# Two-layer mixer behind windowed attention: another order for the first tiles, the first weights and the next block's scores

## The chip, the cores and the metric

The kernel runs on one core of a Trainium2 chip. The metric is the time of one execution on the device in microseconds, the median of several runs. A profiled execution is taken apart, and its trace is what the views show: TensorE (PE, its weight loads PEld), VectorE (DVE), ScalarE (ACT), GpSimd (POOL) and SyncE (SP, which only issues transfers here).

## What is computed

Attention with a causal window of 64 over 4 batches, 8 heads, 576 positions and 64 channels; then two MLP blocks on rows of 512:

```
scores = where(0 <= i - j < 64, q @ k.T / 8, -1e9)
x  = softmax(scores) @ v                        # (4, 576, 512)
xn = (x - mean) / sqrt(var + 1e-6) * g_ln
x  = x + relu(xn @ w_ch1) @ w_ch2               # block "a": 512 -> 2048 -> 512
u  = x + (relu(x.T @ w_tok1) @ w_tok2).T        # over the 576 positions
out = u + relu(u @ w_ch1') @ w_ch2'             # block "b": 512 -> 1536 -> 512
```

All is float32 at the interface. In the MLPs a float32 product is made of three products in a faster format: each operand is split into a high part and a low rest, and high x high, high x low and low x high are summed.

## The kernel before, in words

The 2304 rows lie in 18 tiles of 128. Three tiles make a block of 384 rows, six blocks in all. A tile's attention is done in two units (half of the heads each); unit u belongs to tile u // 2.

The stages of a tile's attention have letters in the string FIRST, which gives the order in which the first three tiles' instructions are issued. S is a tile's scores (L179, 32 small TensorE matmuls into two PSUM tiles, then on VectorE for each unit four masked copies with their maxima, L190), and in the kernel before it ends with the exponentials of both units on ScalarE (`att_E`, L198, four with their sums). T transposes a unit's probabilities on TensorE (L211) and ScalarE copies them out of PSUM (L215) while GpSimd makes the reciprocals of the sums (L217, L218); U does the same with VectorE for the copy (L213) and for the reciprocals (L220, L221). V multiplies with the values (L263) and scales (L265, VectorE). L makes a tile's mean and variance (L271, L272 on VectorE, L273, L274 on GpSimd), N subtracts the mean (L290, VectorE), X transposes the tile's first three column chunks on TensorE (L300) and Y the fourth of all three tiles. E moves a chunk out of PSUM as high part (ScalarE, L317) and low part (VectorE, L318).

Weights come as pieces of 512 KB, in an integer view of 64 bit per value. Sixteen hidden chunks f have two pieces each: (f, 0) for the first product (mm1) and (f, 1) for the second (mm2). A piece goes through four steps: a transfer into one of six raw buffers (L426; the first six on SyncE's queue, the others on ScalarE's), `shrink` on ScalarE (L100; k in FIRST), `narrow` on VectorE (L110, then L113; n), and `split`, with the high part on ScalarE (L92) and the low part on GpSimd (L93; s). Each split issues the transfer of a later piece.

Block 0 of "a" runs over f: mm1 of f (12 matmuls, L351), the narrowing of two pieces, the relu and split of the result (L340 on ScalarE, L341 on VectorE), a list of hooks, then mm2 of f - 2 (nine matmuls, L364). The hooks hold the splits of the two pieces just narrowed, the shrinking of the next two, and the attention of tiles 3 to 5, which are the next block's. Every engine works off its own instructions in the order in which they are issued; the order is written out by hand, and what waits blocks what is behind it on its engine. From block 1 on no weights are prepared until the last block of "a".

Ten products of zeros keep TensorE at work at the very start (`WARM`).

Of the kernel before, what the change touches and what calls it, by code (L numbers as in the profile page):

```python
# [17 lines left out]
P = 128  # L18
# [17 lines left out]

FIRST = ("S0 T0 U1 S1 V0 V1 L0 T2 U3 S2 N0 X0 V2 V3 L1 T4 U5 N1 X1 n1 V4 V5 L2 n1 N2 X2 Y0 s0 E0 E1 E2 E3 k2")


WARM = 10
# [17 lines left out]
def mixer_kernel(ctx, tc, qT, kT, v, g, wa1, wa2, tok1, tok2, wb1, wb2, out):  # L60
# [100 lines left out]
    def att_S(t, lean, first=False):  # L161


        (ba, ia), (bb, _) = tile_blocks(t)
        m_ = masks[:, 1 if ia == 0 else 0]
        wide = [P, NH, 2 * BLK]
        s_ = [ps_a.tile(wide, F32, tag="a", name=f"s{2 * t + hh}") for hh in range(2)]
        for h in range(NH):
            c = slice(h * BLK, (h + 1) * BLK)
            for hh in range(2):  # L170
                r = slice(64 * hh, 64 * hh + 64)
                for s in range(2):
                    if s == 0 and ia == 0:

                        k_ = K[t][r, 1:2, c].to_broadcast([64, 2, BLK])
                    else:
                        j = s if ba == bb else 2 * s
                        k_ = K[t][r, j:j + 2, c]
                    nc.tensor.matmul(s_[hh][64 * s:64 * s + 64, h], lhsT=Q[t][r, s, c], rhs=k_, start=True, stop=True)  # L179
        for hh in range(2):  # L180
            u = 2 * t + hh
            if first:
                f_ = scratch[:, u % KD]
            else:
                f_ = sp.tile(wide, F32, tag="s", name=f"f{u}") if lean else whole[t][:, hh]
            probs[u] = f_
            mx = peak[u] = stp.tile([P, NH, 1], F32, tag="mx", name=f"mx{u}")
            norm[u] = stp.tile([P, NH, 1], F32, tag="sm", bufs=4, name=f"sm{u}") if lean else sums[t][:, hh]
            for h in range(NH):
                nc.vector.tensor_tensor_reduce(out=f_[:, h], in0=s_[hh][:, h], in1=m_, scale=-(D ** -0.5),  # L190
                                               scalar=-2.0 * MASK, op0=ALU.add, op1=ALU.min, accum_out=mx[:, h])
            if lean:
                att_E(u)

    def att_E(u):
# [187 lines left out]
    with tc.manual_schedule():  # L383
# [31 lines left out]
        nc.scalar.activation(out=warm, in_=mhalf, func=AF.Exp)  # L415


        tmps = wslot(FA - 1, [P, 4, DM], "tmps", U32)
        todo = [(0, 0)] + [x for f in range(FA - 1) for x in ((f + 1, 0), (f, 1))] + [(FA - 1, 1)]
        place_of = {x: k for k, x in enumerate(todo)}  # L420
        ready, raws = [], {}

# [14 lines left out]

        def wpairs(n):
            wshrink(n)
            pairs = []  # L440
            for x in ready[:n]:
                k = place_of[x]
                if k < 2 * FA - 3:
                    tmp = tmps[:, k % 4]
                else:
                    tmp = sp.tile([P, DM], U32, tag="s", name=f"tmp{k}")
                pairs.append((tmp, raws.pop(x)))
            return pairs

        def wnarrow(n=1):  # L450
            narrowed.extend((f, i, w) for (f, i), w in zip(ready[:n], narrow(wpairs(n))))
# [12 lines left out]
        for op in LOADS.split():  # L464
            {"q": load_qk, "v": load_v, "g": lambda _: nc.sync.dma_start(out=gsb, in_=g), "w": lambda n: wload(n, nc.sync)}[op[0]](int(op[1:]))

        def first_X(j, c):
            trans_tiles("a", xh, 0, c, (j,), ps_h if c == KD - 1 else ps_acc)

        fns = {"S": lambda t: att_S(t, True, True), "T": lambda u: att_T(u, True),  # L470
               "U": lambda u: att_T(u, True, nc.vector.tensor_copy), "V": att_PV,
               "L": ln_stats, "N": ln_center, "k": wshrink, "n": wnarrow, "s": lambda _: wsplit(False),
               "X": lambda j: [first_X(j, c) for c in range(KD - 1)],
               "Y": lambda _: [first_X(j, KD - 1) for j in range(TPB)], "E": lambda c: evac(c)}
        scratch = xnp.tile([P, KD, NH, P], F32, tag="xn", name="scratch")
        for op in FIRST.split():
            if op == "s0":
                xnt = xnp.tile([P, KD, 2, N], F32R, tag="xn", name="xnt")
            fns[op[0]](int(op[1:]))
        xn = [xnt[:, c] for c in range(KD)]  # L480
# [116 lines left out]
        for i in range(NBLOCKS):  # L597
            hooks = {f: [] for f in range(FA + 2)}
            if i < NBLOCKS - 1:
                u0 = 2 * TPB * (i + 1)  # L600
                lean = i == 0

                def next_qk(t):
                    if t + 1 < NT:
                        place_fixed(t + 1)
                        load_qk(t + 1)

                def next_v(t):
                    if t + 1 < NT:
                        load_v(t + 1)  # L610

                for k in range(2 * TPB if lean else 0):
                    def s1(u=u0 + k):
                        if u % 2 == 0:
                            new_x(u // 2)
                            att_S(u // 2, True)
                            next_qk(u // 2)

                    def s3(u=u0 + k):
                        att_PV(u)  # L620
                        if u % 2 == 1:
                            next_v(u // 2)
                            ln_stats(u // 2)

                    u, t = u0 + k, (u0 + k) // 2
                    hooks[2 * k].append(s1)
                    hooks[2 * k + 2].insert(0, lambda u=u: att_T(u))
                    hooks[2 * k + 3].append(s3)
                    if k % 2 == 1:
                        hooks[2 * k + 4].append(lambda t=t: ln_center(t))  # L630

                def step(op, t, n):
                    if op == "S":
                        new_x(t)
                        tile_S(t)
                        next_qk(t)
                    elif op == "V":
                        tile_PV(t)
                        next_v(t)
                        ln_scalar(t)  # L640
                    else:
                        (tile_T_part if op == "T" else xh_part)(t, n)

                done = collections.Counter()
                for f, ops in enumerate(() if lean else STEPS):
                    for op in ops.split():
                        what, _, n = op.partition("*")
                        for _ in range(int(n or 1)):
                            hooks[f].append(lambda a=(what[0], TPB * (i + 1) + int(what[1]), done[what]): step(*a))
                            done[what] += 1  # L650

                def tr3(i=i):
                    for c in range(3):
                        trans("a", xh, i + 1, c)
                if lean:
                    hooks[FA - 1].append(tr3)

                def after(i=i):
                    if i > 0:
                        for c in range(KD):  # L660
                            for j in range(TPB):
                                gained(c, slice(j * P, (j + 1) * P), uts[TPB * (i + 1) + j][:, c])
                    else:
                        for c in range(3):
                            evac(c)
                        trans("a", xh, i + 1, 3)
                        evac(3)
            else:
                def ysk(k):
                    new_ys(0, k)  # L670
                    for t in range(2 * k, min(2 * k + 2, 9)):
                        y_split(t, nc.vector)
                hooks[0].append(lambda: b_load(3))
                for k in range(5):
                    hooks[k + LAG + 1].append(lambda k=k: ysk(k))
                for f in range(6 + LAG, 13 + LAG):
                    hooks[f - 0.5] = [b_narrow]
                    hooks[f].append(b_split)
                    if f != 7 + LAG:
                        hooks[f] += [b_narrow, b_shrink]  # L680
                hooks[13 + LAG].append(b_split)

                def after():
                    pass
            if i == 0:
                for f in range(FA):
                    if f < FA - 2:
                        hooks[f - 0.5] = [lambda: wnarrow(2)]
                    hooks[f] = hooks[f][:1] + [wsplit] + hooks[f][1:] if f % 2 == 0 else [wsplit] + hooks[f]
                hooks[FA - 2].append(lambda: wnarrow(2))  # L690
            acc = mlp_block("a", i, W, FA, xn, hooks, after)
            for j in range(TPB):
                t = TPB * i + j
                nc.vector.scalar_tensor_tensor(out=xt[t], in0=acc[j], scalar=mv.pop(t)[:, 1:2], in1=xt[t],
                                               op0=ALU.mult, op1=ALU.add)
# [151 lines left out]
```

## Time and profile before

| | us |
|---|---|
| median of three runs | 851.88 |
| the runs | 851.76, 851.88, 854.1 |
| profiled execution | 854.01 |
| its span, first to last instruction | 851.9 |
| TensorE busy | 829.5 (97%) |
| VectorE busy | 525.6 (62%) |
| ScalarE busy | 282.2 (33%) |
| GpSimd busy | 122.5 (14%) |

The busy time of an engine is the time in which one of its instructions runs, waits inside the instruction included. The profiled execution's own time is the span and 2.1 us around it. Time in the trace starts with the span.

### The profile page before, as it was taken

How to read it: one execution, taken by the hardware profiler on the slowest of the kernel's cores; microseconds unless marked ns; L12 is line 12 of the kernel's file. 1: busy time of each engine (PE TensorE's matmuls, PEld its weight loads, DVE VectorE, ACT ScalarE, POOL GpSimd, SP SyncE). 2: the span in 40 equal slices, each digit the busy share in tenths (PEclk: the TensorE clock that was granted, in tenths of full speed). 3: DMA queues.
4: the chain of work that ended last, by engine and by line, in shares of the span. 5: the costliest groups of instructions: out<-in, count | busy, mean ns of one | idle time of the engine just before them, and what ended most of it. 6: DMA issues, size and time to landing. Idle time of an engine off the chain costs nothing.

```text
span 851.9 us, 12974 instructions
## 1 busy us (share of the span) xinstructions
PE 829.5 (97%) x4994; PEld 730.4 (86%) x4994; DVE 525.6 (62%) x1313; ACT 282.2 (33%) x759; POOL 122.5 (14%) x141
## 2 busy tenths in 40 slices
PE   7689999999999999999999999999999999999997
PEld 5578888888888888889999877798999999899996
DVE  4689957787777778777637737985443333344311
ACT  5567634323523432342235431433111111111110
POOL 3365520000000000000004441532000000000000
PEclk9789999999999999999999999999999999999999
DMA  9368512101110110203005400440101010010101
GB/s 328 126 221 266 204 39 79 51 26 63 57 50 26 56 57 25 68 27 99 1 1 155 161 0 25 173 124 0 38 1 38 1 38 0 1 38 1 38 1 37
DMA packets 23213, 58.37 MB, mean 69 GB/s; under 512 B 2800, under 2 KB 3568, under 8 KB 23152
## 3 DMA queue, kind: packets, MB, share of 16 engines
q1 hardware_dynamic: 19408, 43.92, 15.7%
q10 hardware_dynamic: 3744, 13.63, 4.6%
q8 instruction: 39, 0.64, 0.3%
q14 instruction: 22, 0.18, 0.1%
HBM read 52.82 MB, written 4.72 MB: 68 GB/s over the span
## 4 chain that ended last, share of the span: by engine, by line
PE 93%; DVE 3%; issue 1%; ACT 1%; POOL 1%; DVEq 0%; POOLq 0%; ACTq 0%
PE acca L364 24%; PE ha L351 23%; PE hb L351 17%; PE accb L364 17%; PE td L728 2%; PE s L179 2%; PE o L263 2%; PE th L712 1%; DVE ut L326 1%; ACT scratch L198 1%; PE idle L389 1%; PE pt L211 1%; PE king_offset=None)_1_4947 L712 0%; PE king_offset=None)_1_5092 L712 0%; PE king_offset=None)_1_4912 L712 0%
## 5 line engine op out<-in xcount | busy, mean ns | idle before, releaser
L351 PE MATMUL ha<-xnt,wa 128*128 128x384 f32 x1152 | 221.2, 341 | 4.3 <-ACT wa L92 2.4
L351 PEld LDWEIGHTS ha<-xnt,wa 128*128 128x128 f32 x1152 | 206.9, 190 | 13.1 <-ACT wa L92 2.7
L364 PE MATMUL acca<-wa,hTa 128*128 128x512 f32 x864 | 216.8, 397 | 0.0
L364 PEld LDWEIGHTS acca<-wa,hTa 128*128 128x128 f32 x864 | 159.4, 188 | 32.7 <-issue 1.7
L364 PE MATMUL accb<-wb,hTb 128*128 128x512 f32 x648 | 159.1, 392 | 0.0
L364 PEld LDWEIGHTS accb<-wb,hTb 128*128 128x128 f32 x648 | 120.7, 188 | 22.5
L341 DVE SCALAR_TENSOR_TENSOR hTb<-hb,hTb 128x384 fp32r<-128x384 f32 x72 | 40.1, 557 | 150.3 <-ACT hTb L340 150.2
L340 ACT ACTIVATE hTb<-hb 128x384 fp32r<-128x384 f32 x72 | 35.4, 492 | 238.6 <-PE hb L351 238.6
L340 ACT ACTIVATE hTa<-ha 128x384 fp32r<-128x384 f32 x96 | 46.8, 487 | 198.8 <-PE ha L351 198.6
L341 DVE SCALAR_TENSOR_TENSOR hTa<-ha,hTa 128x384 fp32r<-128x384 f32 x96 | 53.1, 554 | 87.6 <-ACT hTa L340 86.0
L239 DVE STREAM_TRANSPOSE pts<-f 32x256 f32<-32x256 f32 x192 | 83.6, 435 | 2.8
L351 PE MATMUL hb<-xnt,wb 128*128 128x384 f32 x432 | 80.9, 337 | 1.1 <-POOL wb L93 0.7
L351 PE MATMUL hb<-us,wb 128*128 128x384 f32 x432 | 80.5, 336 | 0.0
L351 PEld LDWEIGHTS hb<-xnt,wb 128*128 128x128 f32 x432 | 76.4, 188 | 4.4 <-POOL wb L93 1.1
L351 PEld LDWEIGHTS hb<-us,wb 128*128 128x128 f32 x432 | 76.5, 188 | 2.6
L334 DVE STREAM_TRANSPOSE xhT<-xh 32x128 f32<-32x128 f32 x192 | 58.0, 302 | 3.1
L198 ACT ACTIVATE f<-f,mx 128x128 f32<-128x128 f32 x120 | 46.5, 389 | 30.3 <-DVE mx L190 30.3
L326 DVE STREAM_TRANSPOSE ut<-xs 32x384 f32<-32x384 f32 x96 | 54.6, 569 | 1.9
L93 POOL TENSOR_TENSOR wa<-tmps,wa 128x512 fp32r<-128x512 f32 x29 | 40.6, 1423 | 33.1 <-ACT wa L92 33.1
L284 POOL TENSOR_SCALAR mv<-mv 128x1 f32<-128x1 f32 x12 | 2.3, 191 | 276.6 <-ACT xhT L283 276.6
L93 POOL TENSOR_TENSOR wb<-tmpb,wb 128x512 fp32r<-128x512 f32 x24 | 32.3, 1353 | 55.4 <-ACT wb L92 55.4
L728 PE MATMUL td<-h,t 128*128 128x512 f32 x120 | 28.6, 395 | 1.6 <-DVE xs L731 1.6
(115 smaller groups left out, 685.5 us busy)
## 6 DMA issues: line engine op xcount, KB each, us to landing
xs<-in_wa ACTq DMA_DIRECT2D x26, 512.0 KB, 4.2
qkv<-in_wb SPq DMA_DIRECT2D x20, 512.0 KB, 3.8
qkv<-in_v SPq DMA_DIRECT2D x28, 256.0 KB, 2.9
out<-xs SPq DMA_DIRECT2D x16, 256.0 KB, 2.0
qkv<-in_kT SPq DMA_DIRECT2D x10, 384.0 KB, 4.2
qkv<-in_qT SPq DMA_DIRECT2D x14, 256.0 KB, 2.8
xs<-in_wa SPq DMA_DIRECT2D x6, 512.0 KB, 7.9
qkv<-in_kT SPq DMA_DIRECT2D x8, 256.0 KB, 3.0
```

The costliest lines, as they stand in the source:

```text
L93: lo_engine.tensor_tensor(out=dst_lo, in0=src, in1=dst_hi.bitcast(F32), op=ALU.subtract)
L179: nc.tensor.matmul(s_[hh][64 * s:64 * s + 64, h], lhsT=Q[t][r, s, c], rhs=k_, start=True, stop=True)
L198: nc.scalar.activation(out=f_[:, h], in_=f_[:, h], func=AF.Exp, scale=-1.0, bias=mx[:, h], accum_out=sm[:, h])
L239: nc.vector.transpose(out=s_[32 * b:32 * b + 32, :, 32 * a:32 * a + 32], in_=f_[32 * a:32 * a + 32, :, 32 * b:32 * b + 32])
L263: nc.tensor.matmul(o_[r, h], lhsT=p_[:, h, r], rhs=v_[:, s, hh * NH + h, :], start=True, stop=True)
L326: nc.vector.transpose(out=d_[:, :, :, 32 * a:32 * a + 32], in_=s_[:, :, :, 32 * b:32 * b + 32])
L334: nc.vector.transpose(out=uts[t][32 * b:32 * b + 32, :, 32 * a:32 * a + 32], in_=s_)
L340: nc.scalar.activation(out=dst_hi, in_=src, func=AF.Relu)
L341: nc.vector.scalar_tensor_tensor(out=dst_lo, in0=src, scalar=0.0, in1=dst_hi.bitcast(F32), op0=ALU.max, op1=ALU.subtract)
L351: nc.tensor.matmul(h_, lhsT=w[:, a, cs], rhs=src[c][:, b], start=n == 0, stop=n == 3 * KD - 1)
L364: nc.tensor.matmul(acc[j], lhsT=t_[:, a, js], rhs=w[:, 2 + b, :], start=f == 0 and n == 0, stop=f == F - 1 and n == 2)
L728: nc.tensor.matmul(p_, lhsT=t2[tt][:, a, col:col + P], rhs=h1[b][:, tt, c], start=n == 0, stop=n == last)
```

## The change

There are five edits. (1) FIRST is another string: scores are issued earlier, the exponentials have a letter of their own (`e0` to `e5`, one unit each), and the narrowing, shrinking and splitting of the first two weight pieces stand elsewhere. The first tiles' score tiles lie in the PSUM banks of the MLP's accumulators, and their exponentials have six places instead of four. (2) A letter D issues products of the identity with itself into an unused PSUM tile, ten behind V5 and four behind Y0. (3) The pieces are loaded and prepared as mm1 and mm2 use them, so that the two of a step stand the other way round: for f = 0, (2, 0) then (0, 1). (4) Temporaries of the narrowing come from a pool of three pairs. (5) In block 0 tile 3's scores are issued in step 1 instead of 0, those of tiles 4 and 5 in steps 5 and 9 instead of 4 and 8; T follows two steps later for the first unit and three for the second; the splits stand ahead of the scores in each step's hooks, behind a T where there is one.

```diff
-FIRST = ("S0 T0 U1 S1 V0 V1 L0 T2 U3 S2 N0 X0 V2 V3 L1 T4 U5 N1 X1 n1 V4 V5 L2 n1 N2 X2 Y0 s0 E0 E1 E2 E3 k2")
+FIRST = ("S0 e0 e1 S1 e2 T0 U1 e3 S2 V0 V1 L0 e4 T2 U3 e5 N0 X0 V2 V3 L1 T4 U5 k1 N1 X1 V4 V5 L2 n1 D10 N2 X2 Y0 "
+         "k1 D4 s0 n1 E0 E1 E2 E3 s0 k2")
...
-        s_ = [ps_a.tile(wide, F32, tag="a", name=f"s{2 * t + hh}") for hh in range(2)]
+        s_ = [ps_acc.tile(wide, F32, tag="acc", name=f"s{2 * t + hh}") if first else
+              ps_a.tile(wide, F32, tag="a", name=f"s{2 * t + hh}") for hh in range(2)]
...
-                f_ = scratch[:, u % KD]
+                f_ = scratch[:, u]
...
-            if lean:
+            if lean and not first:
                 att_E(u)
...
-        todo = [(0, 0)] + [x for f in range(FA - 1) for x in ((f + 1, 0), (f, 1))] + [(FA - 1, 1)]
+        todo = [(f, 0) for f in range(LAG)] + [x for f in range(FA) for x in ((f + LAG, 0), (f, 1)) if x[0] < FA]
...
+            tmp = ap.tile([P, 2, DM], U32, tag="p", name=f"tmp{place_of[ready[0]]}")
+            return [(tmp[:, k], raws.pop(x)) for k, x in enumerate(ready[:n])]
...
+        def dummies(n):
+            d_ = ps_a.tile([P, DM], F32, tag="a", name=f"idle{n}")
+            for _ in range(n):
+                nc.tensor.matmul(d_[:, 0:P], lhsT=ident, rhs=ident, start=True, stop=True)
...
-                    hooks[2 * k].append(s1)
-                    hooks[2 * k + 2].insert(0, lambda u=u: att_T(u))
-                    hooks[2 * k + 3].append(s3)
+                    u, t, f = u0 + k, (u0 + k) // 2, 4 * (k // 2) + 1
+                    if k % 2 == 0:
+                        hooks[f].append(s1)
+                    hooks[f + 2 + k % 2].insert(0, lambda u=u: att_T(u))
+                    hooks[f + 3 + k % 2].append(s3)
                     if k % 2 == 1:
-                        hooks[2 * k + 4].append(lambda t=t: ln_center(t))
+                        hooks[f + 5].append(lambda t=t: ln_center(t))
...
-                    hooks[f] = hooks[f][:1] + [wsplit] + hooks[f][1:] if f % 2 == 0 else [wsplit] + hooks[f]
+                    n = 1 if f > 0 and f % 4 in (0, 3) else 0
+                    hooks[f] = hooks[f][:n] + [wsplit] + hooks[f][n:]
```

## Rows read from the trace of the kernel before

**Rows 1.** The page: the chain that ended last, shares by engine

```profile
PE 93%; DVE 3%; issue 1%; ACT 1%; POOL 1%; DVEq 0%; POOLq 0%; ACTq 0%
```

**Rows 2.** Stages: start:end, length, busy (xinstructions) by engine, TensorE clock, DMA share, GB/s

```profile
5.94:32.73 26.79, 17.64 (x229) 13.17 (x228) 16.19 (x77) 14.10 (x57) 8.86 (x13) 0.84 0.75 270
32.73:49.86 17.13, 12.82 (x74) 11.14 (x74) 13.10 (x34) 11.54 (x32) 7.39 (x6) 0.70 0.52 175
...
70.82:122.01 51.19, 51.19 (x340) 44.85 (x339) 42.42 (x85) 31.07 (x68) 27.09 (x23) 1.00 0.48 171
```

**Rows 3.** The chain in order of time, 0 to 120: start, us, what

```profile
18.54 0.29 DVE scratch L190
...
20.32 0.41 DVE xh L290
...
26.72 1.59 POOL sm L218
...
31.05 0.49 DVE xh L290
...
32.72 2.19 DVE xnt L318 x4
...
59.98 0.44 PE pt L211 x4
60.42 1.03 PE s L179 x32
...
65.83 0.61 PE o L263 x16
...
68.71 2.11 PE ha L351 x12
...
71.25 2.08 PE acca L364 x9
```

**Rows 4.** Timeline, 34 to 50: start, us, engine line operation tiles [idle before <-releaser]

```profile
35.50 1.29 DVE L113 SCALAR_TENSOR_TENSOR tmps<-xs,tmps 128x512 uint32<-128x512 uint32 x2
...
38.99 0.40 ACT L198 ACTIVATE f<-f,mx 128x128 f32<-128x128 f32 x1 [1.19 <-DVE mx L190]
...
42.10 1.13 ACT L92 ACTIVATE wa<-tmps 128x512 fp32r<-128x512 f32 x2
...
43.28 0.61 PE L351 MATMUL ha<-xnt,wa 128*128 128x384 f32 x2 [2.41 <-ACT wa L92]
...
45.79 3.57 PE L351 MATMUL ha<-xnt,wa 128*128 128x384 f32 x10 [1.90 <-POOL wa L93]
```

**Rows 5.** Timeline of SyncE, 0 to 60: the issue of tile 2's keys

```profile
6.36 0.43 SPq L138 DMA_DIRECT2D kv<-in_kT  x1
```

**Rows 6.** Transfers issued from 6.3 to 6.7: KB, us from issue to landing

```profile
kv<-in_kT SPq DMA_DIRECT2D x1, 384.0 KB, 6.1
```

**Rows 7.** VectorE's groups, 13.5 to 32.7: operation xcount | busy us, mean ns | idle before

```profile
L265 DVE TENSOR_TENSOR xs<-o,sm 128x256 f32<-128x256 f32 x6 | 2.4, 420 | 3.4 <-PE o L263 2.5 <-POOL sm L218 0.9
L271 DVE BATCH_NORM_STATS2 st<-xs 128x6 f32<-128x512 f32 x3 | 2.1, 694 | 0.1
...
L213 DVE COPY pts<-pt 128x512 f32<-128x512 f32 x2 | 1.4, 690 | 0.5 <-PE pt L211 0.5
```

**Rows 8.** Lines L110, L113, L93: count, ns min/median/max, first and last start, shape

```profile
L110 DVE TENSOR_SCALAR tmps<-xs x29: 392/1009/1533, 26.2 to 102.2; 128x512 uint32<-128x512 uint32 x29
...
L113 DVE SCALAR_TENSOR_TENSOR tmps<-xs,tmps x29: 675/679/1776, 26.7 to 103.6; 128x512 uint32<-128x512 uint32 x29
...
L93 POOL TENSOR_TENSOR wa<-tmps,wa x29: 1265/1310/1736, 31.5 to 106.6; 128x512 fp32r<-128x512 f32 x29
```

**Rows 9.** Timeline, 20 to 40: the first mm1

```profile
32.78 4.49 PE L351 MATMUL ha<-xnt,wa 128*128 128x384 f32 x12
```

**Rows 10.** Stages, TensorE alone: start:end, length, busy (xinstructions), clock, DMA share, GB/s

```profile
25.00:30.80 5.80, 1.63 (x35) 1.00 0.31 93
31.00:32.70 1.70, 1.11 (x5) 0.50 0.28 82
```

More of the change, by code (lines that the diff above doesn't have):

```diff
@@ L415, in mixer_kernel @@
         nc.scalar.activation(out=warm, in_=mhalf, func=AF.Exp)
-        tmps = wslot(FA - 1, [P, 4, DM], "tmps", U32)
-        todo = [(0, 0)] + [x for f in range(FA - 1) for x in ((f + 1, 0), (f, 1))] + [(FA - 1, 1)]
+        todo = [(f, 0) for f in range(LAG)] + [x for f in range(FA) for x in ((f + LAG, 0), (f, 1)) if x[0] < FA]
         place_of = {x: k for k, x in enumerate(todo)}
@@ L439, in wpairs @@
             wshrink(n)
[L440 to L448, printed above, removed]
+            tmp = ap.tile([P, 2, DM], U32, tag="p", name=f"tmp{place_of[ready[0]]}")
+            return [(tmp[:, k], raws.pop(x)) for k, x in enumerate(ready[:n])]
         def wnarrow(n=1):
@@ L465, in mixer_kernel @@
             {"q": load_qk, "v": load_v, "g": lambda _: nc.sync.dma_start(out=gsb, in_=g), "w": lambda n: wload(n, nc.sync)}[op[0]](int(op[1:]))
+        def dummies(n):
+            d_ = ps_a.tile([P, DM], F32, tag="a", name=f"idle{n}")
+            for _ in range(n):
+                nc.tensor.matmul(d_[:, 0:P], lhsT=ident, rhs=ident, start=True, stop=True)
         def first_X(j, c):
             trans_tiles("a", xh, 0, c, (j,), ps_h if c == KD - 1 else ps_acc)
-        fns = {"S": lambda t: att_S(t, True, True), "T": lambda u: att_T(u, True),
+        fns = {"S": lambda t: att_S(t, True, True), "e": att_E, "D": dummies, "T": lambda u: att_T(u, True),
                "U": lambda u: att_T(u, True, nc.vector.tensor_copy), "V": att_PV,
@@ L474, in mixer_kernel @@
                "Y": lambda _: [first_X(j, KD - 1) for j in range(TPB)], "E": lambda c: evac(c)}
-        scratch = xnp.tile([P, KD, NH, P], F32, tag="xn", name="scratch")
+        scratch = xnp.tile([P, 2 * TPB, NH, P], F32, tag="xn", name="scratch")
         for op in FIRST.split():
-            if op == "s0":
+            if op == "E0":
                 xnt = xnp.tile([P, KD, 2, N], F32R, tag="xn", name="xnt")
@@ L613, in s1 @@
                     def s1(u=u0 + k):
[L614 to L617, printed above, removed]
+                        new_x(u // 2)
+                        att_S(u // 2, True)
+                        next_qk(u // 2)
                     def s3(u=u0 + k):
@@ L623, in s3 @@
                             ln_stats(u // 2)
-                    u, t = u0 + k, (u0 + k) // 2
-                    hooks[2 * k].append(s1)
-                    hooks[2 * k + 2].insert(0, lambda u=u: att_T(u))
-                    hooks[2 * k + 3].append(s3)
+                    u, t, f = u0 + k, (u0 + k) // 2, 4 * (k // 2) + 1
[3 more added lines that the diff above has]
+                    hooks[f + 3 + k % 2].append(s3)
                     if k % 2 == 1:
-                        hooks[2 * k + 4].append(lambda t=t: ln_center(t))
+                        hooks[f + 5].append(lambda t=t: ln_center(t))
                 def step(op, t, n):
```

## The prediction

> **What bounds the kernel now.** I read the page's shares first: the chain that ended last is 93% TensorE work [rows 1], so time is won only where TensorE stands still or runs at the lower of its two clocks (1.2 instead of 2.4 GHz). The stage table says where that is [rows 2]: from 70.82 to 122.01 us TensorE is busy for all 51.19 us at a granted clock of 1.00; from 32.73 to 49.86 for 12.82 of 17.13 us at 0.70; from 5.94 to 32.73 for 17.64 of 26.79 us at 0.84. Behind some 50 us there is nothing to win, and no line of the change reaches past the first MLP block. So only the first 50 us are worked out, then carried on until both schedules have done the same TensorE work.
>
> In the chain [rows 3] the reader is to see that ahead of 32.7 us it runs through VectorE and GpSimd, with short TensorE pieces between. Behind that point the first block stands: the third mm1 (f=2) gets two matmuls out behind a wait of 2.41 us for ScalarE's copy of its weight, then waits 1.90 more for GpSimd's low half, and goes on at half clock, 3.57 us for ten matmuls where twelve take 2.11 later [rows 3, 4]. ScalarE's lines say why [rows 4]: the exponentials of tile 3 hold it from 38.99 to 42.10, and the copies of the two weight pieces are queued behind them, though the pieces' narrowing on VectorE had ended at 36.8.
>
> **The front.** Scores of tile 1 now go ahead of T0 and U1 on TensorE, those of tile 2 ahead of V0 and V1, and the exponentials (0.39 us each) are placed unit by unit, so that ScalarE no longer alternates with waits for scores. The S tiles lie in three other PSUM banks; s3 takes the bank of s0 when its maxima are read, long before its turn. What binds S2 is data: its keys are issued at 6.36 and land 6.1 us later [rows 5, 6], so S2 runs from 12.5 to 13.6 (1.03 us at full clock, [rows 3]), and its maxima start at 13.6 instead of 18.54.
>
> From 13.6 the front is VectorE's sum. Eight maxima take 1.8 (18.54 to 20.32, [rows 3]); six multiplications 2.5 (0.42 each), three statistics 2.1 with 0.2 for each aggregate, 2.7; two PSUM copies 1.4 and 0.35 for each one's reciprocal, 2.1 [rows 7]; three centerings 1.4 (0.47 to 0.49 each, [rows 3]); narrowing of piece 0, 1.1 (392 and 679 ns, [rows 8]). That is 11.6. To this come two round trips N, X, V through TensorE of 1.2 each (three transposes at 0.11, sixteen PV matmuls at 0.61, four hand-overs) and 0.4 for other hand-overs: 14.4, so N2 ends at 28.0; now it ends at 31.5 (31.05 and 0.49): **3.5 us less**. Of this, 1.1 is the narrowing of piece 1, which now stands behind N2 instead of ahead of it. With S2, X0 and X1 at half clock N2 would end 1.5 later.
>
> New waits: the sums have four buffers, so e4 now waits for V0's multiplication (15.8 us). Behind e4 on ScalarE stand the copy for T2 and e5, and V2 and U5 wait for those. The copy ends at 18.0 and e5 at 19.5, V2's turn on TensorE comes at 19.1 and U5's at 20.8: hidden, with about 1 us to spare. Six scratch slots instead of four take a wait away. GpSimd's power for unit 4, 1.59 us on the chain now (26.72, [rows 3]), ran beside a narrowing that is no longer there; V4's turn comes after it, so it costs nothing here.
>
> **From N2 to the end of the first mm1.** Narrowing of piece 1 starts at 28.0, while GpSimd subtracts piece 0 (copied at 27.6, GpSimd 27.7 to 28.9). The first halves of such narrowings took 392 ns at the least and 1009 in the median, the GpSimd subtraction 1310 [rows 8]; I take the first half as held until 28.9 and the second as free, so it ends at 29.7. The four low halves of the activations follow (2.19, [rows 3]) to 31.9, and mm1 f=0 ends 0.4 later, at 32.3, at full clock. Now it ends at 37.2 [rows 9]: 4.9 earlier, **1.4 us beyond** the 3.5. Bounds: 0.6 earlier if nothing is held, 1.1 later if the second half is held too (its worst is 1776 ns against 679).
>
> The Trainium skill ("SBUF — State Buffer", Who interferes with whom) says that VectorE and GpSimd take one shared pair of ports as an exclusive lock for a whole instruction, VectorE both in its two-port modes and with two SBUF inputs. The trace agrees for the first halves but mostly not for the second, whose median is within 4 ns of its least [rows 8]. By the rule taken literally both halves wait here, and the sum below would be 842.6.
>
> **Dummies.** A 128x128 transpose takes 0.11 us at full clock (four in 0.44, [rows 3]); no row shows a product of the identity with itself. The lower bound is this 0.11, the upper one 0.23, that of a 128x512 product (nine in 2.08): 1.1 to 2.3 us for ten, 0.4 to 0.9 for four. I take 0.11, the row of the same shape. The ten start behind V5 at 25.1 and have until X2 at 28.05; the four end at 29.4 to 29.9, and mm1's second matmul waits for the first low half (30.2) anyway. So they cost nothing at either bound. What they may give is the clock: it was at 0.50 from 31 us on, behind a stretch in which TensorE had been busy for 1.63 of 5.80 us [rows 10], and through the whole first mm1 (4.49 us, [rows 9]). TensorE stood for 3.6 us ahead of that fall; with the ten its longest stand there is 2 us at most. I take full clock; no row bounds it, so half clock is a rival.
>
> **The block.** Within a pair mm1's piece comes first now, and the scores of tile 3 go to step 1, behind the weight copies. Narrowing of pieces 2 and 3 runs on VectorE from 31.9 to 34.1 and the copies follow at once; GpSimd has piece 2 at 34.9 and piece 3 at 36.1. TensorE: mm1 f=1 to 34.4, S to 35.5, mm1 f=2 at once, mm2 f=0 at 37.6, mm1 f=3 at 39.7 (piece 4 at 38.8). The stall is gone. Late next: the exponentials, now from 39.9 to 43.0, hold back the relu of f=2 (43.5) and the copy of piece 6, whose low half comes at 44.9, while mm1 f=4 could start at 44.1: 0.8 us of waiting. Later pieces come in time (piece 8 at 48.8 for 49.9, piece 10 at 52.7 for 55.7).
>
> At the end of mm1 f=6 both have done the same work: now that is at 70.8 (68.71 and 2.11, [rows 3]). From the end of mm1 f=0 it is six mm1 (2.11), four mm2 (2.08), two S (1.03), two T (0.44), two V (0.61): 25.1 us, with the 0.8 and 0.1 of hand-overs 26.0, where the trace has 33.6 (37.2 to 70.8): **7.6 us less**. The two waits of 2.41 and 1.90 and the half clock of f=2's ten matmuls (1.8) make up 6.1 of it, half clock ahead of and behind them the rest.
>
> Off the path: the temporaries move to a pool of three pairs (six pieces instead of four), which adds no wait. Each split issues one load on ScalarE's queue, now some 7 us earlier for pieces 8 and 9; they are shrunk 10 us later. Tile 4's loads on SP's queue go out behind tile 3's scores, as now, and are needed four steps later.
>
> **Sum:** 3.5 + 1.4 + 7.6 = 12.5. The profiled execution took 854.0 (span 851.9 and 2.1 around it), so 841.5. The median of the runs is 851.9: two of three are at 851.8, one at the profiled one's 854.1. These are 2.2 apart, as much as the first mm1 loses at half clock. My sum has no such mm1, so I let 841.5 stand for both; if the 2.2 lie elsewhere it is 839.3.
>
> **Rivals.**
> 1. The clock stays low through mm1 f=0, perhaps f=1: mm1 ends at 34.1 instead of 32.3, and half clock in the front adds up to 1.5, less the 0.8 that is then hidden: 842.5 to 844. For it: the clock is low at 31 us and again at 45.8 [rows 4, 10]; against it the dummies. Chance 0.25.
> 2. The stall only moves: the exponentials ahead of the relu of f=2 cost as much as they do now ahead of the copies. With all 3.1 us of them standing instead of 0.8: 843.8. Against it: TensorE has mm2 f=0, mm1 f=3 and mm2 f=1 to do meanwhile. Chance 0.1.
> 3. The front wins nothing, since VectorE is its bound and only the order changed: 845. For it: 11.6 of 14.4 us are VectorE's. Against it: the maxima of S2 start 4.9 us earlier. Chance 0.06.
> 4. Slower: the preparation becomes the bound of the block. VectorE is busy for 42.42 of 51.19 us there already [rows 2], 4.2 of a step's 5.1. If TensorE starts before the pieces are ahead, and GpSimd holds the second half of both narrowings in every step too (1.1 each), VectorE's step is 6.4 us: 1.3 too many in 13 steps, 17 us, so 858.5. It decides from 6.1 us a step, where the 12.5 are used up. Against it: the second halves are free in most steps. Chance 0.05.
> 5. It doesn't do what it says (no time moved, stalls of the same size elsewhere): 854 or, by the median, 851.9. Chance 0.04.
>
> The forecast keeps 0.5. A measurement of this kernel can tell about 0.3% from no change, 2.6 us: faster 0.91, within it 0.04, slower 0.05. The range goes from 838.5 (the runs' lower level, nothing held) to 846 (rivals 1 and 3 with some of each).
>
> **What would show it.** Right: the maxima of S2 at 13.6, N2's end near 28, mm1 f=0 ending near 32.3 at clock 1.00, no wait over 1 us ahead of mm1 f=2, mm1 f=6 ending near 58. Wrong: mm1 f=0 in over 4 us, waits ahead of mm1 f=4 of over 2 us, a VectorE step of over 6 us, S2 later than 14.5.

## The result, and the profile after

The changed kernel takes 844.59 us, the median of six runs (842.11 to 846.86), beside 851.89 for the kernel before in runs on the same chip (850.15 to 854.1): a ratio of 0.9904 (95%: 0.9887 to 0.992), so 7.3 us less. The forecast was 841.5 in a range of 838.5 to 846. The changed kernel's runs lie on levels that go with the mean granted clock, 842.1 and 842.3 at 1.000, 844.5 to 844.8 at 0.996 and 846.9 at 0.991; the kernel before has levels too, but its mean clock does not order them (850.1 at 0.986, 854.5 at 0.987 in later runs). The profiled execution took 844.72 at 0.996, 9.3 less than the profiled one of before.

The page's first lines, after (span; busy time, share and instructions; shares of the chain that ended last):

```profile
span 842.6 us, 13017 instructions
...
PE 824.9 (98%) x5022; PEld 728.8 (86%) x5022; DVE 524.5 (62%) x1313; ACT 282.0 (33%) x759; POOL 119.5 (14%) x141
...
PE 90%; DVE 3%; issue 1%; ACT 1%; POOL 0%; DVEq 0%; ACTq 0%
```

The stages after, cut at the events the forecast named (end of N2, end of mm1 f=0, end of mm1 f=6; columns as in [rows 2]), and under them the last two stages between the same events before:

```profile
5.94:29.37 23.43, 16.44 (x243) 14.02 (x242) 15.18 (x75) 12.57 (x54) 6.82 (x12) 0.85 0.76 285
29.37:34.31 4.94, 4.13 (x27) 3.72 (x28) 4.84 (x10) 3.90 (x8) 2.62 (x3) 1.00 0.60 213
34.31:61.86 27.55, 26.36 (x214) 23.02 (x213) 26.66 (x66) 20.72 (x50) 16.03 (x13) 1.00 0.75 254
61.86:113.11 51.25, 51.25 (x341) 45.13 (x341) 44.10 (x91) 33.70 (x84) 26.18 (x23) 1.00 0.49 178
```

```profile
31.53:37.27 5.74, 5.68 (x22) 4.91 (x23) 4.07 (x9) 3.40 (x7) 2.50 (x3) 0.50 0.26 91
37.27:70.82 33.55, 29.24 (x215) 25.62 (x215) 27.84 (x70) 23.26 (x64) 17.97 (x14) 0.89 0.67 218
```

The reader is to see three things. N2 ends 2.2 us earlier (31.53 to 29.37), the stretch from there to the end of mm1 f=0 is 0.8 shorter and at full instead of half clock, and the six steps from f=0 to f=6 are 6.0 shorter: 9.0 of the pair's 9.3, where the forecast had 3.5, 1.4 and 7.6. From 61.86 on TensorE is again busy all the time, as before [rows 2]. And in the block VectorE is now busy for 26.66 of 27.55 us, the time in which it waits inside an instruction included.

The timeline after, at the places where a term came out otherwise than forecast (columns as in [rows 4]):

```profile
9.71 2.00 PE L181 MATMUL s<-kv,q 64*64 64x128 f32 x32 [2.42 <-DMA kv<-in_kT]
...
11.64 1.92 PE L213 MATMUL pt<-ident,scratch 128*128 128x128 f32 x8
13.49 1.10 PE L181 MATMUL s<-kv,q 64*64 64x128 f32 x32
...
19.80 1.66 PE L265 MATMUL o<-kv,pts 128*64 128x64 f32 x32
21.39 1.97 PE L213 MATMUL pt<-ident,scratch 128*128 128x128 f32 x8
...
26.38 2.50 PE L464 MATMUL idle<-ident 128*128 128x128 f32 x20
...
29.72 1.27 POOL L94 TENSOR_TENSOR wa<-tmp,wa 128x512 fp32r<-128x512 f32 x1 [0.31 <-ACT wa L93]
29.81 1.73 DVE L114 SCALAR_TENSOR_TENSOR tmp<-xs,tmp 128x512 uint32<-128x512 uint32 x1
...
47.32 2.01 PE L353 MATMUL ha<-xnt,wa 128*128 128x384 f32 x10 [0.53 <-POOL wa L94]
...
49.99 2.54 POOL L94 TENSOR_TENSOR wa<-tmp,wa 128x512 fp32r<-128x512 f32 x2 [1.29 <-ACT wa L93]
50.24 1.07 DVE L222 TENSOR_SCALAR sm<-sm 128x4 f32<-128x4 f32 x1
...
56.39 1.09 PE L181 MATMUL s<-qkv 64*64 64x128 f32 x28 [0.65 <-DVE xs L267]
```

S1 and the transposes behind it ran at half clock (2.00 and 1.92 us), so did T4 and U5 (1.97) and part of V2 and V3 (1.66). The second half of piece 1's narrowing was held beside GpSimd's subtraction. In the block a wait of 0.53 and one of 0.65 are left where waits of 2.41 and 1.90 stood [rows 4].

### The profile page after: what moved, and what is told of

Read it like the earlier page. It is cut to its first block, busy times and chain, and to the rows that moved or that the text cites. A ratio compares the mean times of both kernels' runs of the same rounds, so it can differ in the third digit from the quotient of the medians.

```text
span 842.6 us, 13017 instructions
## 1 busy us (share of the span) xinstructions
PE 824.9 (98%) x5022; PEld 728.8 (86%) x5022; DVE 524.5 (62%) x1313; ACT 282.0 (33%) x759; POOL 119.5 (14%) x141
## 4 chain that ended last, share of the span: by engine, by line
PE 90%; DVE 3%; issue 1%; ACT 1%; POOL 0%; DVEq 0%; ACTq 0%
PE acca L366 23%; PE ha L353 23%; PE hb L353 18%; PE accb L366 17%; PE td L728 2%; PE o L265 2%; PE s L181 2%; PE th L712 1%; DVE ut L328 1%; PE king_offset=None)_1_4976 L712 0%; PE king_offset=None)_1_5121 L712 0%; PE king_offset=None)_1_4941 L712 0%; DVE us L94 0%; DVE xs L731 0%; DVE xs L799 0%
## 5 line engine op out<-in xcount | busy, mean ns | idle before, releaser
L353 PE MATMUL ha<-xnt,wa 128*128 128x384 f32 x1152 | 217.4, 337 | 1.3 <-DVE xnt L320 0.7
L353 PEld LDWEIGHTS ha<-xnt,wa 128*128 128x128 f32 x1152 | 203.7, 188 | 9.9 <-DVE xnt L320 1.0
L94 POOL TENSOR_TENSOR wa<-tmp,wa 128x512 fp32r<-128x512 f32 x32 | 42.2, 1339 | 34.6 <-ACT wa L93 34.6
```

The lines of the kernel that those rows point to most:

```text
L94: lo_engine.tensor_tensor(out=dst_lo, in0=src, in1=dst_hi.bitcast(F32), op=ALU.subtract)
L353: nc.tensor.matmul(h_, lhsT=w[:, a, cs], rhs=src[c][:, b], start=n == 0, stop=n == 3 * KD - 1)
```

## The experiments

Two theories on the whole: the parts add up, with the block as the larger (mine); or most of it is the clock that the dummies keep (the rival). Later ones ask what bounds the shortened block, and what the front lost. One table for all: three events in the profiled execution, the stretch between the last two, and the median of the timed runs with its ratio to the kernel before, which ran beside each (851.9 and, with e5 to e8, 852.3).

| kernel | N2 ends | mm1 f=0 ends | mm1 f=6 ends | f=0 to f=6 | median us | ratio (95%) |
|---|---|---|---|---|---|---|
| before | 31.53 | 37.27 | 70.82 | 33.55 | 851.9 | |
| after | 29.37 | 34.31 | 61.86 | 27.55 | 844.59 | 0.9904 (0.9887 to 0.992) |
| e1_block_only | 30.43 | 35.75 | 63.2 | 27.45 | 846.07 | 0.9932 (0.9911 to 0.9952) |
| e2_front_only | 29.68 | 34.61 | 67.16 | 32.55 | 849.63 | 0.9974 (0.996 to 0.9987) |
| e3_no_dummies | 28.78 | 35.41 | 62.54 | 27.1 | 845.79 | 0.9931 (0.9912 to 0.995) |
| e4_old_pieces | 29.08 | 34.01 | 61.9 | 27.9 | 844.70 | 0.9918 (0.9896 to 0.9941) |
| e5_short_narrow | 28.59 | 33.54 | 59.19 | 25.65 | 841.95 | 0.9872 (0.9855 to 0.9889) |
| e6_scores_first | 28.13 | 33.08 | 60.22 | 27.14 | 843.96 | 0.9901 (0.9881 to 0.992) |
| e7_more_dummies | 27.01 | 31.96 | 59.48 | 27.52 | 842.44 | 0.9884 (0.9869 to 0.9899) |
| e8_early_pieces | 27.69 | 31.59 | 59.20 | 27.6 | 842.22 | 0.9882 (0.9864 to 0.99) |
| e9_dummies_scores | 27.15 | 32.09 | 59.25 | 27.16 | 842.26 | 0.9879 (0.9863 to 0.9896) |
| e10_pool_recip | 27.71 | 32.66 | 59.13 | 26.47 | 841.81 | 0.9876 (0.9857 to 0.9895) |
| e11_one_early | 28.58 | 33.02 | 61.40 | 28.4 | 843.91 | 0.9893 (0.9873 to 0.9913) |

After, e4, e5 and e6 have the same front; N2 ends in them between 28.13 and 29.37. So one profiled execution tells fronts apart only from about 1.2 us on. The stretch f=0 to f=6 is the steadier column: e6 and e9, with the same block, have 27.14 and 27.16, the changed kernel and e7 27.55 and 27.52.

**e1, the block alone**: the kernel before with the new places of the hooks.

```diff
-hooks[2 * k].append(s1)
+f = 4 * (k // 2) + 1
+if k % 2 == 0: hooks[f].append(s1)
...
+n = 1 if f > 0 and f % 4 in (0, 3) else 0
+hooks[f] = hooks[f][:n] + [wsplit] + hooks[f][n:]
```

> The kernel before with the block's hooks of the changed kernel alone (scores of tiles 3 to 5 a step later, splits ahead of them); its front and its order of pieces stay. Theory (the parts add up, and this is the larger one): the exponentials no longer stand ahead of the weight copies, so the waits of 2.41 and 1.90 us ahead of mm1 f=2 shrink to under 1 us together (the low half of its piece is GpSimd's second, so about 1 us may stay), the low clock behind them goes too, and from the end of mm1 f=0 to the end of mm1 f=6 it is about 28 instead of 33.6 us; the front is as before (N2 ends at 31.5). Time 5 to 6 us below the kernel before, some 846 to 847. Rival (the stall is set by when narrowing starts, which only the new front moves): under 1.5 us gained, and the wait ahead of mm1 f=2 stays over 3 us.

5.9 us less than before, as expected. Its TensorE timeline shows f=0 still slow. Ahead of f=2 only 0.41 of the waits of 2.41 and 1.90 is left, and ahead of f=4 a wait of 0.84 stands (the lines are f=0 with f=1, then the last ten matmuls of f=2 and of f=4):

```profile
31.67 6.17 PE L351 MATMUL ha<-xnt,wa 128*128 128x384 f32 x24
...
39.83 2.00 PE L351 MATMUL ha<-xnt,wa 128*128 128x384 f32 x10 [0.41 <-POOL wa L93]
...
49.73 2.01 PE L351 MATMUL ha<-xnt,wa 128*128 128x384 f32 x10 [0.84 <-POOL wa L93]
```

N2 ended at 30.43 and not at 31.5, though the front is that of the kernel before: S1 took 1.10 us in this execution and 1.99 in the profiled one of before, full and half clock.

**e2, the front alone**: the changed kernel with the old places of the hooks (e1's edit reversed).

> The changed kernel with the hooks of the kernel before (scores of tile 3 in step 0, ahead of the splits); front, dummies, order of pieces and pool of temporaries stay changed. Theory (the parts add up): N2 ends near 29.4, mm1 f=0 near 34.3 at full clock, then the stall ahead of mm1 f=2 is there as before, 3 to 4 us, and with it the low clock: 2.5 to 4 us below the kernel before, 848 to 849.5. Rival (the front's head start is lost in the stall, since the exponentials of tile 3 end when they end): within 1 us of the kernel before.

2.3 us less than before, a little under the 2.5 to 4 expected, and the stall is back, with half clock behind it:

```profile
41.21 1.01 PE L353 MATMUL ha<-xnt,wa 128*128 128x384 f32 x2 [3.28 <-ACT wa L93]
42.57 3.57 PE L353 MATMUL ha<-xnt,wa 128*128 128x384 f32 x10 [0.36 <-POOL wa L94]
```

5.9 and 2.3 make 8.2, where the whole gave 7.3 and, by intervals, 6.8 to 9.6: the parts add, and the block is the larger. With the earlier front alone TensorE stands for 3.64 us (3.28 and 0.36) where it stood for 4.31 [rows 4]: without the hooks the stall stays.

**e3, no dummies.**

```diff
-n1 D10 N2 X2 Y0 k1 D4 s0 n1
+n1 N2 X2 Y0 k1 s0 n1
```

> The changed kernel without its fourteen dummy products (both letters D taken out). Theory (they hold the clock): the clock falls to 0.50 near 31 us as in the kernel before, mm1 f=0 takes over 4 us from its first matmul and ends near 36, of which the block's later waits hide up to 1 us: 1 to 2 us above the changed kernel in the profile, 845.5 to 846.5. Rival (they do nothing, the shorter waits of TensorE alone keep the clock): mm1 f=0 ends at 34.3 as with them, time within 0.5 us of the changed kernel.

The clock falls in mm1 f=0, as in the kernel before [rows 9], behind a wait of TensorE of 2.98 us for N2 (TensorE alone; columns as in [rows 10]):

```profile
29.91:35.41 5.50, 4.57 (x15) 0.50 0.49 183
35.41:62.54 27.13, 26.50 (x214) 0.99 0.78 262
```

It costs 1.2 us by the medians, though the two intervals overlap. The way from N2 to the end of mm1 f=0 is 1.7 longer (6.63 after 4.94); the stretch behind it gives 0.4 back (27.1 after 27.55). So in these profiles the dummies keep the clock of mm1 f=0, and they are a small part of the gain.

**e4, the pieces in the old order** inside a pair.

```diff
-todo = [(f, 0) for f in range(LAG)] + [x for f in range(FA) for x in ((f + LAG, 0), (f, 1)) if x[0] < FA]
+todo = [(0, 0)] + [x for f in range(FA - 1) for x in ((f + 1, 0), (f, 1))] + [(FA - 1, 1)]
```

> The changed kernel with the pieces of a step in the old order, mm2's first. Theory (what gates mm1 is the low half that GpSimd makes, and it comes second here, 1.3 us later): mm1 f=2 waits about 1.1 us more, mm1 f=4 1.3 more (0.53 now), together 2 to 2.5 us above the changed kernel, about 847. Rival (pieces are ready early enough in either order): within 0.5 us of the changed kernel.

My expectation fell: no difference that can be told. There are waits where I expected them, smaller (0.52 ahead of f=2; 1.16 instead of 0.53 ahead of f=4),

```profile
38.20 2.02 PE L353 MATMUL ha<-xnt,wa 128*128 128x384 f32 x10 [0.52 <-POOL wa L94]
...
48.45 2.01 PE L353 MATMUL ha<-xnt,wa 128*128 128x384 f32 x10 [1.16 <-POOL wa L94]
```

but the wait of 0.65 ahead of the scores is gone, and the stretch is 27.9 instead of 27.55. In sum the waits grew by 0.5 and the stretch by 0.35, where 2 to 2.5 were expected. Most of what TensorE waits more in one place it waits less in another, so something else sets the stretch.

**e5, the second narrowing operation on a quarter of its columns** in the first six steps (the weights of those steps are then not the reference's).

```diff
-narrow(wpairs(n))
+narrow(wpairs(n), cols=DM // 4 if 2 <= k < 14 else None)
```

> The changed kernel with the second half of the narrowing (the shift and or) done for 128 of 512 columns only, for the twelve pieces of steps 0 to 5; those weights are not the reference's. Theory (between the end of mm1 f=0 and the end of mm1 f=6 VectorE is the bound, busy for 26.7 of 27.6 us, and TensorE's waits only show where it is late): 0.8 us less VectorE work a step, the wait of 0.53 ahead of mm1 f=4 and the 0.65 inside the scores of tile 4 both go, the stretch takes 25.5 to 26.2 us, 1.3 to 2 us below the changed kernel. Rival (the two waits have causes of their own, exponentials ahead of the relu and a PSUM bank): the stretch stays within 0.5 us of 27.6.

The stretch after the first mm1 in e5 (columns as in [rows 2]):

```profile
33.54:59.19 25.65, 25.65 (x213) 22.90 (x213) 23.95 (x71) 21.04 (x55) 17.05 (x14) 1.00 0.81 270
```

TensorE is busy for all of it, and 1.9 us are gone though only VectorE's work was cut: VectorE's lateness sets the shortened block, down to TensorE's own 25.65 us. That is the point of rival 4, at a much smaller size.

**e6, scores of the next tiles ahead of the V that follows them**, since the wait of 0.65 stood ahead of S for VectorE's multiplication, whose operand shares a PSUM bank.

```diff
-hooks[f].append(s1)
+hooks[f].insert(len(hooks[f]) - (1 if k else 0), s1)
```

> The changed kernel with the scores of tiles 4 and 5 issued ahead of V of the tile before, in the same hooks, so that they take the banks of the two T tiles and not the one that V's late multiplication still reads. Theory (VectorE is the bound): the wait of 0.65 us inside the scores of tile 4 goes, another comes in its place, end of mm1 f=6 within 0.4 us of 61.9 and time within 0.5 us of the changed kernel. Rival (the PSUM bank is a cost of its own): 0.7 to 1.1 us less.

```profile
55.17 0.69 PE L265 MATMUL o<-qkv,pts 128*64 128x64 f32 x16 [0.61 <-DVE xs L267]
...
33.08:60.22 27.14, 26.00 (x214) 22.86 (x213) 26.29 (x68) 21.16 (x53) 15.75 (x12) 1.00 0.72 251
```

The wait moved to V (0.61), as the theory had it, and 0.4 us went from the stretch; the median is 0.6 lower, which lies between theory and rival and can't be told from nothing.

**e7, more dummies in the front**: eight behind S0 and nine behind U3, because S1, T0 and U1 ran at half clock.

```diff
-S0 e0 e1 S1 e2 T0 U1 ... T2 U3 e5 N0
+S0 D8 e0 e1 S1 e2 T0 U1 ... T2 U3 D9 e5 N0
```

> The changed kernel with dummies also where TensorE waits in the front: eight behind S0, nine behind U3. Theory (the front was later than forecast because S1, T0 and U1 ran at half clock): the clock stays at 1.00 through S1, T0 and U1, S2 starts near 13.0, set by its keys, instead of 13.5, T4 and U5 take 1 us instead of 2, N2 ends at 28.0 to 28.6 instead of 29.4: 0.8 to 1.4 us below the changed kernel in the profile. Rival (VectorE's own sum binds the front): N2 within 0.4 us of 29.4.

The same part of the front, first in the changed kernel (TensorE alone, as in [rows 10]), then in e7, with S1 and S2 in its timeline and, under them, its stages (columns as in [rows 2]):

```profile
9.70:13.40 3.70, 3.69 (x40) 0.54 1.05 404
```

```profile
9.21 1.22 PE L181 MATMUL s<-kv,q 64*64 64x128 f32 x32 [0.56 <-DMA kv<-in_kT]
12.29 1.22 PE L181 MATMUL s<-kv,q 64*64 64x128 f32 x32 [0.83 <-DVE mx L192]
...
9.20:13.40 4.20, 3.35 (x72) 2.84 (x72) 2.64 (x19) 3.66 (x18) 0.96 (x1) 1.00 1.04 396
27.01:31.96 4.95, 4.14 (x27) 3.73 (x28) 4.85 (x9) 3.90 (x8) 2.62 (x3) 1.00 0.63 210
31.96:59.48 27.52, 26.33 (x213) 23.02 (x213) 26.64 (x66) 21.39 (x53) 16.03 (x13) 1.00 0.74 256
```

Full clock, S2 at 12.29 instead of 13.49 and no longer right behind TensorE's own work, N2's end 2.4 us earlier, which is 1 to 1.6 better than expected, and everything behind it as in the changed kernel (4.95 and 27.52, after 4.94 and 27.55). The profile names VectorE's maxima as what S2 waited for; S2's keys land then too (issued at 6.37, 5.8 us to landing, so at 12.17), and which of the two held it is not shown. The median is 2.1 less (1.7 by the ratios to the kernel before, as e5 to e8 ran on another chip), with overlapping intervals. The clock is the steadier evidence: from 9.2 to 24 us its mean is 0.75 to 0.88 in the six profiles without these dummies (the changed kernel, e2 to e6) and 1.00 in the four of e7 to e10. So the front's missing part was the clock.

**e8, pieces 0 and 1 narrowed earlier**, between the front's own VectorE work, on top of e7.

```diff
-L0 e4 ... X0 V2 ... N1 X1 V4 V5 L2 n1 D10 N2 X2 Y0 k1 D4 s0 n1 E0 ... E3 s0 k2
+L0 k1 e4 ... X0 n1 s0 V2 ... N1 X1 n1 V4 V5 D7 s0 k2 L2 N2 X2 Y0 E0 ... E3
```

> The changed kernel with another FIRST: dummies as in the run with more of them, both pieces narrowed in VectorE's two waits for TensorE (behind X0 and behind X1), split there too, and pieces 2 and 3 shrunk ahead of the activations' high parts; seven dummies instead of ten behind V5 and none behind Y0. Theory (1.1 us of narrowing sits on the path to N2, and 2.2 with 1.0 of holding between N2 and the first low half): N2 ends near 27.5, the first low half starts under 1 us behind the first high half, mm1 f=0 ends near 31.5 to 32.3 instead of 34.3, and 1.5 to 3 us are kept at the end, as VectorE's stretch behind it only moves: 841.5 to 843. Rival (narrowing and subtraction beside GpSimd's powers slow the chain to V4, and the clock falls with fewer dummies ahead of mm1): within 0.7 us of the changed kernel.

From N2 to the end of mm1 f=0 it takes 3.90 instead of 4.95, but N2 ends no earlier (27.69, in e7, e9 and e10 27.01 to 27.71) though two pieces' narrowing was to fill idle time there: the multiplications now wait for GpSimd. V2's waits for a power that ran beside the narrowing and took 1.58 us (1.04 in e7). V4's power took 1.05 as ever, but came late: GpSimd had the subtraction of piece 0 ahead of it, and the addition before the power took 0.73 beside the second narrowing (0.29 in e7). GpSimd's lines, then VectorE's:

```profile
18.52 1.58 POOL L220 TENSOR_TENSOR sm<-sm,mone 128x4 f32<-128x4 f32 x1
21.19 1.27 POOL L94 TENSOR_TENSOR wa<-tmp,wa 128x512 fp32r<-128x512 f32 x1 [1.09 <-ACT wa L93]
...
23.57 0.73 POOL L219 TENSOR_SCALAR sm<-sm 128x4 f32<-128x4 f32 x1
24.39 1.05 POOL L220 TENSOR_TENSOR sm<-sm,mone 128x4 f32<-128x4 f32 x1
...
20.13 0.76 DVE L267 TENSOR_TENSOR xs<-o,sm 128x256 f32<-128x256 f32 x2 [0.94 <-POOL sm L220]
...
25.47 0.76 DVE L267 TENSOR_TENSOR xs<-o,sm 128x256 f32<-128x256 f32 x2 [1.26 <-POOL sm L220]
```

The events and the time (842.22) came out as the theory had them, but e7's dummies alone give as much: of the earlier narrowing 0.2 is left in the median, which is nothing that can be told.

**e9, e7 and e6 together.**

> The changed kernel with both edits that stood alone before: dummies in the front, and scores ahead of V in the block. Theory (front bound by VectorE and its start, the stretch from mm1 f=0 to f=6 bound by VectorE): the front's 2 us and the stretch's 0.5 add up, 841.5 to 842.5; N2 ends near 27. Rival (what the front gives is eaten by the stretch): 843.5 or more.

The sum of the two events holds (N2 at 27.15, stretch 27.16), the median is e7's within 0.2, and its five runs all lie within 0.5 us at a clock of 0.999 to 1.000, where those of the changed kernel spread over 4.7. That the dummies narrow the spread is not shown: e4's four runs, without them, lie within 0.2.

**e10, e9 with the block's softmax reciprocals on GpSimd** instead of VectorE, to take the 1.07 us operation away.

```diff
-if first and not copy:
+if not copy:
```

> The run with dummies and scores first, and in block 0 the reciprocals of the sums made by GpSimd instead of VectorE (two VectorE instructions of 1.07 and 0.18 us a unit go, GpSimd gets 1.3 us a unit). Theory (VectorE bounds the stretch; its 1.07 is mostly held by GpSimd's subtraction): about 1.2 us less VectorE in each of two units, the stretch 0.5 to 1.5 us shorter, 840.5 to 841.5. Rival (GpSimd's reciprocals delay its subtractions and V's multiplication, as they do in the front): same time or up to 1 us more.

The stretch of e9 and that of e10 (columns as in [rows 2]):

```profile
32.09:59.25 27.16, 26.03 (x214) 22.89 (x213) 26.28 (x68) 21.30 (x53) 15.71 (x12) 1.00 0.72 246
```

```profile
32.66:59.13 26.47, 25.93 (x214) 22.86 (x213) 25.56 (x57) 20.22 (x48) 19.92 (x16) 1.00 0.73 249
```

The stretch is 0.7 shorter, at the low end of what was expected; the median is 0.45 lower, 0.3 above the expected range and too little for two such medians to tell. VectorE is busy for 0.7 less too, where 2.4 was expected, but that is not the same work done faster. The four instructions that went took 2.5 in e9, while the second narrowing operations grew by 4.2 us, the first ones took 1.6 less, and other work of VectorE now falls behind the stretch's end. The second operations in e9, then in e10 (count, busy us and mean ns, idle before):

```profile
L114 DVE SCALAR_TENSOR_TENSOR tmp<-xs,tmp 128x512 uint32<-128x512 uint32 x12 | 8.8, 771 | 0.0
...
L114 DVE SCALAR_TENSOR_TENSOR tmp<-xs,tmp 128x512 uint32<-128x512 uint32 x12 | 13.0, 1120 | 0.1
```

What went on TensorE is the wait ahead of V. This is the version with the lowest median among those with the whole computation: 841.81, 10.1 us below the kernel before and 2.8 below the changed one.

**e11, only piece 0 narrowed earlier**, on top of e9, to keep e8's gain without its loss.

```diff
-L0 e4 ... X0 V2 ... k1 N1 X1 V4 V5 L2 n1 D10 N2 X2 Y0 k1 D4 s0 n1 E0 ... E3 s0 k2
+L0 k1 e4 ... X0 n1 s0 V2 ... k3 N1 X1 V4 V5 D10 L2 N2 X2 Y0 n1 E0 ... E3 s0
```

> The run with dummies and scores first, with piece 0 narrowed and split in VectorE's wait behind X0, piece 1 narrowed behind N2 (no subtraction of GpSimd is then beside it), and pieces 1 to 3 shrunk early. Theory (of what lies between N2 and the end of mm1 f=0, 1.0 is holding by GpSimd's subtraction of piece 0, and 1.1 ahead of N2 is the narrowing of piece 0): piece 1's second half takes 0.69 instead of 1.73, mm1 f=0 ends 1 to 1.5 us earlier than in the run it is built on, 840 to 841.5. Rival (the narrowing beside GpSimd's power of unit 2 slows V2's multiplication by as much, or VectorE's stretch takes it back): within 0.5 us of that run.

The theory fell. The later narrowing is free now, with no subtraction beside it, but V2's multiplication waits as in e8, and the clock falls ahead of V4 and V5 (VectorE, TensorE, then the stage):

```profile
20.84 0.76 DVE L267 TENSOR_TENSOR xs<-o,sm 128x256 f32<-128x256 f32 x2 [0.94 <-POOL sm L220]
...
29.02 0.69 DVE L114 SCALAR_TENSOR_TENSOR tmp<-xs,tmp 128x512 uint32<-128x512 uint32 x1
...
24.66 1.98 PE L265 MATMUL o<-kv,pts 128*64 128x64 f32 x32
...
24.00:27.20 3.20, 3.20 (x38) 0.51 0.29 108
```

1.65 us slower than e9, more than the rival's 0.5: N2 ends 1.4 later, the way to the end of mm1 f=0 is 0.5 shorter as was hoped, and the stretch behind it is 1.2 longer.

## Why the prediction was right, and where its sum was not

The direction, the place and the mechanism held: the stall of the third mm1 went because the exponentials no longer stand ahead of the weight copies (e1, e2), the front moved earlier, mm1 f=0 runs at full clock (1.00 from 29.37 to 34.31), and nothing behind the block changed. The time is 3.1 us above the forecast, and the sum was 3.5 too good (12.5 against 9.0 at the end of mm1 f=6): three terms were mis-sized.

**The front, 2.2 instead of 3.5.** The step that was off is "S2 runs from 12.5 to 13.6". It named the keys as what binds S2 and left out S1, which waited 2.42 us for keys of its own and then, like the transposes behind it, ran at half clock (2.00 and 1.92 us). S2 stood behind TensorE itself and began at 13.49, and its maxima at 14.63 instead of 13.6. From there to N2's end the changed kernel took 14.7 us, near the 14.4 of the sum. That is luck: at full clock the same way takes 13.6 (13.41 to 27.01 in e7), so the sum had it 0.8 too long, and the second fall of the clock, from V2 to U5, which it did not have, cost 1.1. The forecast priced half clock in the front (S2, X0 and X1, 1.5 us) but left it to the first rival.

**From N2 to the end of mm1 f=0, 0.8 instead of 1.4.** I took the second half of piece 1's narrowing as free, since its median was within 4 ns of its least [rows 8]. It took 1.73 us beside GpSimd's subtraction (29.72 to 30.99); e11, with none beside it, shows 0.69. I had put that subtraction one operation earlier, beside the first half; it began when ScalarE's copy was there, and then the second half was due. The median of 29 said nothing of what lies beside this one. The first half, which I had as held, ran free (0.42), so the net loss is 0.5; mm1 f=0 ended 0.7 instead of 0.4 behind the last low half, and that is the rest. Here the literal reading of the Trainium skill ("SBUF — State Buffer", Who interferes with whom: one shared pair of ports as an exclusive lock, taken also by a VectorE operation with two SBUF inputs) was the better one, and the trace now agrees with it for this operation too (1.73 us beside a subtraction, 0.69 without).

**The block, 6.0 instead of 7.6.** The forecast had 25.1 us of TensorE work, 0.1 of hand-overs and one wait of 0.8, for which it named ScalarE's exponentials. The trace has 27.55, with 0.53 ahead of mm1 f=4 and 0.65 ahead of S, for GpSimd and VectorE. Those two waits are only 0.4 above the 0.8, so they don't explain the 1.6. e5, in which TensorE never stands, divides it: 25.65 us are TensorE's own time, 0.45 above the sum's, and 1.9 is lost to VectorE's lateness, 1.1 above the sum's 0.8, some of it as time in which TensorE counts as busy. So what the sum lacked most is VectorE as the bound of this stretch: I had priced it as a rival of 17 us, decided from 6.1 us a step, and not as a small loss below that point. e4 and e6 show that moving TensorE's order mostly moves the waits.

**One forecast for profile and median.** I put the 2.2 us between the runs of the kernel before down to the first mm1 and let 841.5 stand for both. e1 speaks against it: with the same front, mm1 f=0 is slow too and yet ends 1.5 earlier than in the profiled execution of before, 1.1 of it ahead of N2's end. So a part of the 2.2 lies in the front, and the profiled pair, 9.3 us apart, flatters the change; the medians say 7.3.

**The dummies** cost nothing on the path, as said, though ten took 2.50 us (0.25 each; the trace has two records for one product), just above the upper bound of 0.23. That they are needed is e3's 1.2 us; the chance of 0.25 for a low clock went to the wrong place: it was low in S1 and again from V2 to U5, not in mm1 f=0. The two of six runs at a mean clock of 1.000 took 842.1 and 842.3, within 0.8 of the forecast.

What stays open: why the clock falls in S1 in some executions and later in others. The wait ahead of S1 alone does not decide it: S1 ran at full clock (1.22 us) behind waits of 2.97 us in e5 and 3.23 in e6, and at half clock behind 2.42 in the changed kernel. Open too is whether e10 is below e9 at all, and by what way its stretch became shorter.

## What to carry to other kernels

When a stall goes, add up each engine's work over the shortened stretch before you list which wait is late next: VectorE, 83% busy beside the stall, set the pace without it. A median over a kernel's instructions doesn't price one of them: ask what lies beside this one. And where a front hangs on other engines and the clock falls in TensorE's waits, TensorE work that nobody needs can keep it up there too, not only ahead of the large products.

## What the runs showed of the hardware

A tiny VectorE operation is held like a large one: the 128x4 addition took 0.16 us alone and 1.07 beside a subtraction on GpSimd, to whose end it ran both times in the changed kernel; the reciprocal behind it took 0.18 beside the next subtraction. GpSimd pays too: a 128x4 power that started just behind a narrowing on VectorE took 1.58 us in e8, and 1.04 without one in e7. A product of the 128x128 identity with itself took 0.25 us at full clock, more than twice a transpose of the same shape (0.11, [rows 3]).
